# Longer allowances, an earlier division and two engines for one copy in an attention stage that a planner lays out

## The chip, the cores and the metric

The kernel runs on one core of one Trainium2 chip. The metric is the device time of one execution in microseconds (us). Of the kernel before there are three timed runs and one profiled execution. TensorE is called PE here, VectorE DVE, ScalarE ACT, GpSimd POOL and SyncE SP, as in the profile; PEld is PE's weight load and SPq is SP as it issues DMAs.

## What is computed

One token mixer over 2048 tokens of width 576: sliding-window attention with 32 heads of width 18 and a window of 256, times a gate that comes from a gMLP.

```python
def _A_ref(x, wqkv, wo):                  # H = 32, Dh = 18, W = 256
    q, k, v = ...                         # x @ wqkv, by heads
    scores = einsum("bhqd,bhkd->bhqk", q, k) * (Dh ** -0.5)
    mask = (i - j >= 0) & (i - j < W)
    p = softmax(where(mask, scores, -1e9))
    o = einsum("bhqk,bhkd->bhqd", p, v)
    return o.transpose(0, 2, 1, 3).reshape(B, S, D) @ wo

def _B_ref(x, w_in, w_sp, b_sp, w_out):
    z = gelu(x @ w_in)
    z1, z2 = z[..., :Fh], layernorm(z[..., Fh:])
    g = einsum("ts,bsf->btf", w_sp, z2) + b_sp[None, :, None]
    return (z1 * g) @ w_out

xn = layernorm(x)
return x + _A_ref(xn, ...) * silu(_B_ref(xn, ...))
```

## The kernel before

The program has five stretches: the projections to q, k, v and z2; the attention stage (about 425 to 875 us of the span); the output projection `wo`; the large product with `w_sp`; and the product with `w_out`. Products are computed with operands split into a high and a low part, three matmuls for one. The change touches the attention stage alone.

**Units.** Attention runs over 16 units (`UNITS`, numbered 0 to 15, `NU` = 16): four heads by one half of the tokens each. The q and k rows of two heads (a pair, two per unit) lie in one of six slots, the tiles `att0` to `att5`. Eight DMAs per pair bring them from `st_d` (L552, `pair_jobs`). `open_unit(u)` runs when all scores of unit u-1 have been laid out; it spaces the loads for unit u+2 by `LOAD_STEP` = 700 ns and notes in `head_ready` that a pair may be used `LOAD_NS` after its last load. Unit 0 opens three pairs (3, 4, 5) at once, with an extra delay.

**What a unit does.** `max_item` (L619, L623) computes scores of 128 queries against up to 384 keys, and VectorE takes their maxima. `max_split` and `max_turn` (L634, L643, L649) turn the unit's maxima round into the tile `mhl`, and four small DMAs put them into the slots as two more rows (L656). `scores` (L751, L755) computes the scores once more, transposed and with the maxima taken off, and ScalarE takes the exponential into `pt`. GpSimd zeroes the corners of `pt` that lie outside the window (the masks, `affine_select`, L764 and L767). `pv` (L780) multiplies by the values into the bank `ops`, which ScalarE copies to `ou` (L795). `finish` then divides by the sums of the exponentials: the sums go out as `den` (L852), VectorE inverts them (L825), they go to `r_d` (L827) and come back spread over partitions into the tile `rp` (L832; there is one `rp` buffer for units 0 to 14), GpSimd multiplies in four parts (L836), and four DMAs store the rows to `o_d` (L841). `INVERT_AT`, `FETCH_AT` and `DIVIDE_AT` say when, counted from the unit's end. The last unit but one (14) has shorter delays, and the last (15) is divided in the next stretch.

**Fill.** Between those, PE computes the product z1 of the gMLP (`z1_rows`, L696): 18 blocks of weights (`z1raw`, L666, split on ScalarE and GpSimd at L712), two halves of the array's rows that work side by side, 27 matmuls to a bank. When a bank is complete ScalarE copies it to one of three `z1o` buffers (L701), and SP stores that to `z1_d` (L590; the profile calls it `z_d`), `KEEP_NS` later in the plan.

**What sets the order.** The whole stage is laid out by a planner that runs while the program is built. It keeps a clock and, for each engine, the time until which it is busy (`use`, `busy`), at estimated costs; it gives PE the next thing whose inputs it takes to be ready, `GUARD` ns after their estimated end: a `pv` run, a turn of maxima, a score, a maximum, or else a z1 matmul. DMAs and delayed work wait in a list (`after`, `tick`). The result is one fixed order for each engine. On the chip each engine follows its order and waits for semaphores, SP too: a DMA that must wait holds all DMAs behind it. DMAs take eight semaphores in turn, so a DMA also waits until the eighth before it has landed.

Of the kernel before, what the change touches and what calls it, by code (L numbers as in the profile page):

```python
# [11 lines left out]
AF = mybir.ActivationFunctionType  # L12
# [19 lines left out]
HS = S // 2  # L32
SLOT = HS + HS + 256
UNITS = [(g, half) for half in range(2) for g in range(8)]
NU = len(UNITS)
# [4 lines left out]
RMN = 16  # L40
QR = 5
STEPS = 27
GUARD = 150
LOAD_NS = 7500
MAX_NS = 8500
KEEP_NS = 2000
LOAD_STEP = 700
INVERT_AT = 11000
FETCH_AT = 8000
# [19 lines left out]
def kernel(  # L69
# [14 lines left out]
    act, dve, pool, pe, sp = nc.scalar, nc.vector, nc.gpsimd, nc.tensor, nc.sync  # L84
# [14 lines left out]
    r_d = dram.tile([NU, 4, HS], F32, name="r_d")  # L99
# [139 lines left out]
    with ExitStack() as early:  # L239
# [282 lines left out]
        with ExitStack() as ph:  # L522
# [34 lines left out]
            clock = 0.0  # L557
            row_time = [0.0, 0.0]

            def after(ns, fn):  # L560
                waiting.append((clock + ns, fn))
# [19 lines left out]
            def use(engine, ns, drain=0):  # L581

                busy[engine] = max(busy[engine], clock + 200) + ns
                return busy[engine] + drain
# [79 lines left out]
            def load_z1(f):  # L664
                raw = zw.tile([P, 9, P], F32, name="z1raw", bufs=1)
                sp.dma_start(raw, w_z1[f])  # L666
                wh, wl = (zw.tile([P, 9, P], F32R, name=n) for n in ("z1wh", "z1wl"))

                jobs = []
                for ks in (slice(0, 3), slice(3, 6), slice(6, 9)):  # L670
                    jobs.append((partial(act.activation, wh[:, ks], raw[:, ks], AF.Copy), "act", 420))
                for ks in (slice(0, 3), slice(3, 6), slice(6, 9)):
                    jobs.append((partial(pool.tensor_tensor, wl[:, ks], raw[:, ks], f32(wh[:, ks]), ALU.subtract),
                                 "pool", 1000))
                return wh, wl, jobs

            z1w = {}
# [5 lines left out]
            def z1_rows(r):  # L683

                for f in range(FH // P):
                    z1_at[r] = f
                    if f not in z1w:
                        z1w[f] = load_z1(f)
                    wh, wl, jobs = z1w[f]
                    while jobs:  # L690
                        jobs.pop(0)[0]()
                    for b in range(2):
                        bank, ps = take()
                        bank_of[r] = bank
                        for n, (w, x_) in enumerate(moving_x(wh, wl, slice(b * 512, (b + 1) * 512), r)):
                            pe.matmul(ps, w, x_, start=n == 0, stop=n == STEPS - 1)  # L696
                            spend(r, MM + 3)
                            z1_done[r] += 1
                            if n == STEPS - 1:
                                zo = zw.tile([P, 512], F32, name="z1o", bufs=3)  # L700
                                act.activation(zo, ps, AF.Copy)  # L701
                                bank_of[r] = None
                                bank_free[bank] = use("act", 480, 120) + 100
                                after(bank_free[bank] - clock + KEEP_NS,
                                      partial(sp.dma_start, z1_tokens[f * P:(f + 1) * P, b, :, r],
                                              zo.rearrange("p (a q) -> p a q", a=2)))
                            if f + 1 < FH // P and min(z1_at) == f:
                                if b == 0 and n == 0 and f + 1 not in z1w:
                                    z1w[f + 1] = load_z1(f + 1)
                                if b == 1 and n % 4 == 2 and f + 1 in z1w and z1w[f + 1][2]:  # L710
                                    job, engine, ns = z1w[f + 1][2].pop(0)
                                    job()  # L712
                                    use(engine, ns)
                            yield
# [21 lines left out]
            def scores(u, kb, qa, qz, j):  # L736
                half = UNITS[u][1]
                lo = 8 * half
                base = 0 if half == 0 else 6
                if (u, kb) not in pts:  # L740
                    pts[u, kb] = ap_.tile([P, 4, 384], F32, name="pt", bufs=PTB)
                    left[u, kb] = 4
                pt = pts[u, kb]
                left[u, kb] -= 1
                n = qz - qa + 1
                a = qa
                if n == 1:
                    a = qa - 1 if qa > lo else qa
                m = max(n, 2)
                bank, ps = take()  # L750
                pe.matmul(ps[:, :m * P], k_of(u, j)[:, (kb - base) * P:(kb - base + 1) * P],  # L751
                          q_of(u, j)[:, (a - lo) * P:(a - lo + m) * P], start=True, stop=True)
                spend(j % 2, MM * m / 4 + 4)
                d0 = (qa - kb) * P
                act.activation(pt[:, j, d0:d0 + n * P], ps[:, (qa - a) * P:(qa - a + n) * P], AF.Exp, scale=scale)  # L755
                done_exp.append(use("act", 53 + 106 * n, 125))
                bank_free[bank] = done_exp[-1] + GUARD
                if not left[u, kb]:
                    todo.append([done_exp[-1] + 200, u, kb, qa, qz])
                    for cut in (qa == kb, qz == kb + 2):  # L760
                        busy["pool"] = max(busy["pool"], todo[-1][0]) + 600 * cut
                    todo[-1][0] = busy["pool"] + 100
                    if qa == kb:
                        pool.affine_select(out=pt[:, :, 0:P], in_=pt[:, :, 0:P], pattern=[[0, 4], [1, P]],  # L764
                                           compare_op=ALU.is_ge, fill=0.0, base=0, channel_multiplier=-1)
                    if qz == kb + 2:
                        pool.affine_select(out=pt[:, :, 256:384], in_=pt[:, :, 256:384], pattern=[[0, 4], [-1, P]],  # L767
                                           compare_op=ALU.is_gt, fill=0.0, base=0, channel_multiplier=1)
# [40 lines left out]
            def finish(u, ou):  # L809
# [6 lines left out]
                def rp():  # L816
# [4 lines left out]
                                  f32(slots[4][:, 0:HS]))  # L821
                    return at[0]

                def invert():
                    dve.reciprocal(den, den)  # L825
                    t = use("dve", 270) - clock + 300
                    after(t + (1500 if u < NU - 2 else 300), lambda: sp.dma_start(r_d[u].rearrange("h (a b) -> (h a) b", b=HS // 32), den))  # L827
                    for i in range(4):
                        after(t + (FETCH_AT if u < NU - 2 else 4500) + 400 * i, partial(sums, i))

                def sums(i):
                    sp.dma_start(rp()[32 * i:32 * i + 32, :], r_d[u][i:i + 1, :].to_broadcast([32, HS]))  # L832
# [1 line left out]
                def divide(a, n=4):  # L834
                    hs = slice(a * HS // n, (a + 1) * HS // n)
                    pool.tensor_tensor(ou[:, hs], ou[:, hs], rp()[:, hs], ALU.mult)  # L836
                    use("pool", 2900 / n)

                def store(i):
                    h = 4 * g + i  # L840
# [2 lines left out]
                if u == NU - 1:  # L843
                    def put_last():
                        dve.reciprocal(den, den)
                        sp.dma_start(r_d[u].rearrange("h (a b) -> (h a) b", b=HS // 32), den)

                    last.extend([lambda: sp.dma_start(den, ou[DH::32, :]), put_last,
                                 lambda: [sums(i) for i in range(4)], lambda: [divide(a, 2) for a in range(2)],
                                 lambda: [store(i) for i in range(4)]])  # L850
                else:
                    after(busy["act"] - clock + 1000, lambda: sp.dma_start(den, ou[DH::32, :]))  # L852
                    sooner = 10000 if u == NU - 2 else 0
                    after(4500 if sooner else INVERT_AT, invert)
                    parts[u] = [partial(divide, a) for a in range(4)] + [partial(store, i) for i in range(4)]
                    for ns in DIVIDE_AT:
                        after(ns - (14500 if sooner else 0), partial(part, u))

            def sp_combos(stack):

# [180 lines left out]
            with ExitStack() as heads:  # L1041
# [23 lines left out]
                def open_unit(u):  # L1065

                    pairs = (2 * u + 4, 2 * u + 5) if u else (3, 4, 5)
                    jobs = [(p, it) for p in pairs if p < 2 * NU for it in [pair_jobs(p)] for _ in range(8)]
                    for i, (p, it) in enumerate(jobs):
                        ns = 300 + LOAD_STEP * i + (4000 if u == 0 else 0)  # L1070
                        after(ns, partial(next, it, None))
                        head_ready[p] = clock + ns + LOAD_NS

# [680 lines left out]
```

## Time and profile before

| | |
|---|---|
| median of 3 runs | 1839.44 us (1839.17 to 1839.54) |
| profiled execution, its own time | 1837.79 us |
| its span, from first to last instruction | 1836.0 us |
| granted TensorE clock, mean | 0.994 |
| first and last z1 matmul of the attention stage (PE) | 425.4 and 872.3 us |
| POOL busy, in all | 430.5 us (23%) |

The page's first part gives each engine's busy time and share. Its second part cuts the span into 40 slices; PE is at 9 tenths in all but a few, among them those at about 440, 600 and 850 us. The windows ask for the same by chosen stretches: columns are the stretch, its length, then busy time and number of instructions of PE, PEld, DVE, ACT and POOL, then the granted PE clock, the DMA engines' share and GB/s. Matmuls overlap in PE, so a window of 10.00 busy can still hide gaps shorter than a matmul's 0.4 us. A row of the waits reads: engine, tile and line, what it waited for, us in total, times, longest. In a timeline the last bracket gives the idle time before an instruction and what ended it.

### The profile page before, as it was taken

To read this page: it belongs to the slowest core of one execution; us is meant where nothing else is said; L and a number is where in the kernel's file an instruction comes from. 1 tells how busy PE (TensorE), PEld (TensorE's weight loads), DVE (VectorE), ACT (ScalarE), POOL (GpSimd) and SP (SyncE) were. 2 spreads that over 40 slices of the span, in tenths; PEclk is the share of its full clock that TensorE was granted. 3 is DMA by queue.
4 is the path that set the end of the run, shared out by engine and by line. 5 is a ranking of instruction groups with operands and counts; after the bars stand their busy time and mean duration, and the time that the engine had idled before them with its cause. 6 is when DMAs were issued, how large, how long until landed. Compare 5 with 4: busy or idle time off the path is not lost.

```text
span 1836.0 us, 37716 instructions
## 1 busy us (share of the span) xinstructions
PE 1806.0 (98%) x14373; PEld 1591.3 (87%) x14373; DVE 1127.9 (61%) x2299; ACT 938.6 (51%) x1757; POOL 430.5 (23%) x507
## 2 busy tenths in 40 slices
PE   8999999999999999998999999999999999999998
PEld 8999999998778777776988888888888888899998
DVE  7321333457577666751266687667876567767876
ACT  5433322223767666775467565465454544444443
POOL 3332333343455555665000000112100000000000
PEclk9999999999999999999999999999999999999999
DMA  8785688887567777755867777699786556787554
GB/s 276 188 227 170 227 277 285 279 263 245 156 168 192 192 192 189 200 150 163 269 233 233 251 222 265 238 306 307 239 270 233 179 186 198 249 263 208 154 160 136
DMA packets 266917, 405.73 MB, mean 221 GB/s; under 512 B 52336, under 2 KB 180592, under 8 KB 266608
## 3 DMA queue, kind: packets, MB, share of 16 engines
q1 hardware_dynamic: 266736, 403.32, 71.7%
q8 instruction: 113, 1.85, 0.4%
q14 instruction: 68, 0.56, 0.1%
HBM read 285.35 MB, written 117.09 MB: 219 GB/s over the span
## 4 chain that ended last, share of the span: by engine, by line
PE 83%; DMA 6%; DVE 5%; SPq 2%; ACT 2%; issue 1%; POOL 1%; DVEq 0%; ACTq 0%; POOLq 0%
PE acc L1493 34%; PE mb L209 11%; PE c L1585 8%; PE ma L209 5%; PE ops L780 4%; PE s L696 3%; PE wops L1212 3%; PE t L696 3%; PE mb L696 2%; PE ma L696 2%; SPq L366 1%; PE s L619 1%; DMA att<-st_d 1%; DMA st_d<-qkhl 1%; DMA wraw<-in_w_qk_dram 1%
## 5 line engine op out<-in xcount | busy, mean ns | idle before, releaser
L1493 PE MATMUL acc<-spl,zh 128*128 128x512 f32 x1008 | 392.6, 390 | 0.9 <-DVE spl L119 0.5
L1493 PE MATMUL acc<-sph,zl 128*128 128x512 f32 x1008 | 392.2, 389 | 0.0
L1493 PE MATMUL acc<-sph,zh 128*128 128x512 f32 x1008 | 392.1, 389 | 0.0
L119 DVE TENSOR_TENSOR spl<-spr,sph 128x1024 fp32r<-128x1024 f32 x168 | 210.2, 1251 | 39.4 <-ACT sph L118 37.7
L1493 PEld LDWEIGHTS acc<-spl,zh 128*128 128x128 f32 x1008 | 189.2, 188 | 41.7 <-DVE spl L119 2.6
L1493 PEld LDWEIGHTS acc<-sph,zh 128*128 128x128 f32 x1008 | 189.2, 188 | 39.6
L1493 PEld LDWEIGHTS acc<-sph,zl 128*128 128x128 f32 x1008 | 189.2, 188 | 38.9
L118 ACT ACTIVATE zh<-b 128x384 fp32r<-128x384 f32 x168 | 87.4, 520 | 209.9 <-PE acc L1493 209.8
L118 ACT ACTIVATE sph<-spr 128x1024 fp32r<-128x1024 f32 x168 | 176.0, 1048 | 13.0 <-DMA spr<-in_w_sp_dram 5.3
L119 DVE TENSOR_TENSOR zl<-b,zh 128x384 fp32r<-128x384 f32 x168 | 99.6, 593 | 124.5 <-ACT zh L118 124.5
L623 DVE CUSTOM_DVE_ANT_0 s<-s,band 128x384 f32<-128x384 f32 (+2 forms) x256 | 136.6, 560 | 47.8 <-PE s L619 31.8
L696 PE MATMUL s<-b,z1wh 64*128 64x512 f32 x504 | 148.6, 397 | 0.2 <-ACT z1wh L712 0.2
L1585 PE MATMUL c<-b,o 128*128 128x288 f32 x1056 | 144.6, 296 | 1.7 <-DVE o L119 0.9
L1585 PEld LDWEIGHTS c<-b,o 128*128 128x128 f32 x1056 | 141.8, 189 | 2.2 <-DVE o L119 1.1
L987 DVE BATCH_NORM_STATS2 st<-zt 128x6 f32<-128x384 f32 x96 | 49.3, 548 | 131.5 <-ACT zt L986 131.1
L755 ACT ACTIVATE pt<-s 128x384 f32<-128x384 f32 (+2 forms) x252 | 108.4, 462 | 37.8 <-PE s L751 25.3
L696 PE MATMUL t<-b,z1wh 64*128 64x512 f32 x378 | 124.3, 403 | 0.0
L209 PE MATMUL ma<-z2w,b 64*128 64x384 f32 x648 | 116.1, 333 | 0.0
L209 PE MATMUL mb<-z2w,b 64*128 64x384 f32 x648 | 116.0, 333 | 0.0
L209 PE MATMUL mb<-att,b 64*128 64x384 f32 x648 | 112.8, 331 | 0.0
L209 PE MATMUL ma<-att,b 64*128 64x384 f32 x648 | 112.8, 331 | 0.0
L209 PEld LDWEIGHTS mb<-z2w,b 64*128 64x128 f32 x648 | 112.4, 184 | 0.0
(260 smaller groups left out, 4797.8 us busy)
## 6 DMA issues: line engine op xcount, KB each, us to landing
spr<-sc_d SPq DMA_DIRECT2D x96, 512.0 KB
spr<-in_w_sp_dram SPq DMA_DIRECT2D x72, 512.0 KB
zr<-z_d SPq DMA_DIRECT2D x144, 192.0 KB
z_d<-zt SPq DMA_DIRECT2D x48, 384.0 KB
z_d<-z1o SPq DMA_DIRECT2D x72, 256.0 KB
z1t<-z_d SPq DMA_DIRECT2D x72, 256.0 KB
y_d<-z1t SPq DMA_DIRECT2D x72, 256.0 KB
a<-in_w_sp_dram SPq DMA_DIRECT2D x64, 256.0 KB
```

Of the source, the lines that this page charges most:

```text
L118: act.activation(hi, src, AF.Copy)
L119: dve.tensor_tensor(lo, src, f32(hi), ALU.subtract)
L209: pe.matmul(banks[h][:, :n], *both[h][i], start=i == 0, stop=i == STEPS - 1)
L366: sp.dma_start(rows[c].rearrange("i h a p -> (i h) a p"), f32(hl[64 * n:64 * n + 64, c]).rearrange("q (a p) -> q a p", a=2))
L623: dve.tensor_tensor_reduce(out=ps[:, :w], in0=ps[:, :w], in1=band[:, m0:384], scale=1.0, scalar=-3.0e38, op0=ALU.add, op1=ALU.max, accum_o ...
L696: pe.matmul(ps, w, x_, start=n == 0, stop=n == STEPS - 1)
L755: act.activation(pt[:, j, d0:d0 + n * P], ps[:, (qa - a) * P:(qa - a + n) * P], AF.Exp, scale=scale)
L780: pe.matmul(o_ps[c][32 * j:32 * j + 32, (qa - 4 * c) * P:(hi - 4 * c + 1) * P], vgs[u][:, kb - k0, j * VW:j * VW + 32], pt[:, j, (qa - kb) ...
L987: dve.bn_stats(st2[:, s, pc, :], zv)
L1212: pe.matmul(po[:, i, :288], lt[:, cs], r[:, i * 288:(i + 1) * 288], start=n == 0, stop=n == len(pl) - 1)
L1493: pe.matmul(acc[j], z[:, ps], w[:, cs], start=s == i == 0 and n in OPENS, stop=s == 7 and i == 2, skip_group_check=True)
L1585: pe.matmul(banks[key][:, :288], y, w, start=begin and k == n == 0, stop=close and k == 8 and n == 2, skip_group_check=True)
```

## The change

It changes estimates and delays of the planner, lets a z1 copy go to either of two engines, and gives unit 13 (the third last) delays of its own:

- `GUARD` 150 to 200 ns, `LOAD_NS` 7500 to 9500 ns, and the extra delay of unit 0's loads 4000 to 7000 ns.
- Estimated costs on GpSimd: a mask 600 to 640 ns, a quarter of a weight split 1000 to 1020, a unit's division 2900 to 2960.
- A finished z1 bank is copied by VectorE when the planner expects that to end sooner (its cost taken as 620, ScalarE's as 480).
- `early` is 0 for units 0 to 12 and 15, 1 for unit 13, 2 for unit 14. Unit 14 keeps its delays. Unit 13 is inverted 7000 ns after its end instead of 11000, its inverted sums are fetched 6000 ns after that instead of 8000, and its divisions and stores come 8000 ns sooner.

```diff
-GUARD = 150
-LOAD_NS = 7500
+GUARD = 200
+LOAD_NS = 9500
...
-                                act.activation(zo, ps, AF.Copy)
                                 bank_of[r] = None
-                                bank_free[bank] = use("act", 480, 120) + 100
+                                if max(busy["dve"], clock + 200) + 620 < max(busy["act"], clock + 200) + 480:
+                                    dve.tensor_copy(zo, ps)
+                                    bank_free[bank] = use("dve", 600, 140) + 100
+                                else:
+                                    act.activation(zo, ps, AF.Copy)
+                                    bank_free[bank] = use("act", 480, 120) + 100
...
-                        busy["pool"] = max(busy["pool"], todo[-1][0]) + 600 * cut
+                        busy["pool"] = max(busy["pool"], todo[-1][0]) + 640 * cut
...
+                early = max(u - NU + 4, 0) if u < NU - 1 else 0
+
                 def invert():
                     dve.reciprocal(den, den)
                     t = use("dve", 270) - clock + 300
-                    after(t + (1500 if u < NU - 2 else 300), lambda: sp.dma_start(r_d[u]...
+                    after(t + (1500, 600, 300)[early], lambda: sp.dma_start(r_d[u]...
                     for i in range(4):
-                        after(t + (FETCH_AT if u < NU - 2 else 4500) + 400 * i, partial(sums, i))
+                        after(t + (FETCH_AT, 6000, 4500)[early] + 400 * i, partial(sums, i))
...
-                    use("pool", 2900 / n)
+                    use("pool", 2960 / n)
...
-                    sooner = 10000 if u == NU - 2 else 0
-                    after(4500 if sooner else INVERT_AT, invert)
+                    after((INVERT_AT, 7000, 4500)[early], invert)
...
-                        after(ns - (14500 if sooner else 0), partial(part, u))
+                        after(ns - (0, 8000, 14500)[early], partial(part, u))
...
-                        ns = 300 + LOAD_STEP * i + (4000 if u == 0 else 0)
+                        ns = 300 + LOAD_STEP * i + (7000 if u == 0 else 0)
```

Since the planner decides everything by its clock, the order of all engines differs from the opening of the stage to its end. The instructions are the same, but for 15 of the 72 z1 copies, which are now on VectorE. Three places follow, in the words of the built program (line, operation, output and inputs, shape; the line numbers of the changed kernel are up to five higher).

SP at the opening of the stage, right after the values of unit 0 (`vg`); `att_6802` is the slot of pair 3, `mhl` holds unit 0's maxima, `z1o` a finished z1 bank. Before:

```order
L666 DMA z1raw<-in_w_z_dram 128x1152
L552 DMA att_6802<-st_d 36x1024
L552 DMA att_6802<-st_d 18x1024 x2
L552 DMA att_6802<-st_d 36x1024
L656 DMA att_2212<-mhl 2x8x128 x2
L656 DMA att_2213<-mhl 2x8x128 x2
L552 DMA att_6802<-st_d 36x1024
L552 DMA att_6802<-st_d 18x1024 x2
L590 DMA z_d<-z1o 128x2x256
```

Now:

```order
L666 DMA z1raw<-in_w_z_dram 128x1152
L656 DMA att_2212<-mhl 2x8x128 x2
L656 DMA att_2213<-mhl 2x8x128 x2
L552 DMA att_6802<-st_d 36x1024
L552 DMA att_6802<-st_d 18x1024 x2
L590 DMA z_d<-z1o 128x2x256 x2
L552 DMA att_6802<-st_d 36x1024 x2
```

The maxima stand ahead of pair 3's eight loads, and the first two z1 stores after three of these instead of seven and eight.

POOL at the end of the stage, with buffer numbers; `ou_13389` is unit 13's result before and `ou_13822` unit 14's, now `ou_13519` and `ou_13925`. Before:

```order
L836 TENSOR_TENSOR ou_13389<-ou_13389,rp_13996 128x256 x4
L764 AFFINE_SELECT pt_14054<-pt_14054 128x4x128
L767 AFFINE_SELECT pt_14054<-pt_14054 128x4x128
L836 TENSOR_TENSOR ou_13822<-ou_13822,rp_14081 128x256
L764 AFFINE_SELECT pt_14098<-pt_14098 128x4x128
L767 AFFINE_SELECT pt_14098<-pt_14098 128x4x128
L836 TENSOR_TENSOR ou_13822<-ou_13822,rp_14081 128x256
L764 AFFINE_SELECT pt_14137<-pt_14137 128x4x128
L836 TENSOR_TENSOR ou_13822<-ou_13822,rp_14081 128x256 x2
L764 AFFINE_SELECT pt_14168<-pt_14168 128x4x128
```

Now, two pieces of the same queue:

```order
L842 TENSOR_TENSOR ou_13519<-ou_13519,rp_13831 128x256 x2
L771 AFFINE_SELECT pt_13959<-pt_13959 128x4x128
L842 TENSOR_TENSOR ou_13519<-ou_13519,rp_13831 128x256
L768 AFFINE_SELECT pt_13980<-pt_13980 128x4x128
L771 AFFINE_SELECT pt_13980<-pt_13980 128x4x128
L842 TENSOR_TENSOR ou_13519<-ou_13519,rp_13831 128x256
```

```order
L771 AFFINE_SELECT pt_14141<-pt_14141 128x4x128
L768 AFFINE_SELECT pt_14179<-pt_14179 128x4x128
L768 AFFINE_SELECT pt_14214<-pt_14214 128x4x128
L842 TENSOR_TENSOR ou_13925<-ou_13925,rp_14221 128x256 x4
L842 TENSOR_TENSOR att5_13914<-att5_13914,att4_6804 128x512 x2
```

Unit 13's divisions have moved ahead of the last unit's masks, and unit 14's behind all of them. The last row is unit 15, divided in the next stretch.

PE at the end of the z1 matmuls; each bank belongs to one half of the array's rows. Before, the last matmuls of bank `s0` with the last one of `ma` ahead of them:

```order
L696 MATMUL ma_14252<-b2_93,z1wl_13746 128x512
L696 MATMUL s0_14263<-b2_93,z1wl_13746 128x512
L696 MATMUL s0_14263<-b2_93,z1wh_13745 128x512
L696 MATMUL s0_14263<-b5_96,z1wh_13745 128x512
L696 MATMUL s0_14263<-b2_93,z1wl_13746 128x512
```

Now the last matmul of `ma` and the first of those of `t1` behind it:

```order
L696 MATMUL ma_14105<-b2_93,z1wl_13618 128x512
L696 MATMUL t1_14272<-b1_92,z1wl_13618 128x512
L696 MATMUL t1_14272<-b1_92,z1wh_13617 128x512
L696 MATMUL t1_14272<-b4_95,z1wh_13617 128x512
L696 MATMUL t1_14272<-b1_92,z1wl_13618 128x512
```

After the first matmul of the remaining half, which runs beside the last one of `ma`, three stood alone before; now there are fifteen.

More of the change, by code (lines that the diff above doesn't have):

```diff
@@ L673, in load_z1 @@
                     jobs.append((partial(pool.tensor_tensor, wl[:, ks], raw[:, ks], f32(wh[:, ks]), ALU.subtract),
-                                 "pool", 1000))
+                                 "pool", 1020))
                 return wh, wl, jobs
@@ L826, in invert @@
                     t = use("dve", 270) - clock + 300
-                    after(t + (1500 if u < NU - 2 else 300), lambda: sp.dma_start(r_d[u].rearrange("h (a b) -> (h a) b", b=HS // 32), den))
+                    after(t + (1500, 600, 300)[early], lambda: sp.dma_start(r_d[u].rearrange("h (a b) -> (h a) b", b=HS // 32), den))
                     for i in range(4):
-                        after(t + (FETCH_AT if u < NU - 2 else 4500) + 400 * i, partial(sums, i))
+                        after(t + (FETCH_AT, 6000, 4500)[early] + 400 * i, partial(sums, i))
                 def sums(i):
```

## The prediction

> **What bounds the kernel now.** I read the page first, then the windows of 10 us over the attention stage, then the waits, the chain and single engines' timelines.
>
> ```profile
> PE 1806.0 (98%) x14373; PEld 1591.3 (87%) x14373; DVE 1127.9 (61%) x2299; ACT 938.6 (51%) x1757; POOL 430.5 (23%) x507
> PE 83%; DMA 6%; DVE 5%; SPq 2%; ACT 2%; issue 1%; POOL 1%; DVEq 0%; ACTq 0%; POOLq 0%
> ```
>
> TensorE (PE) is the bound: busy 98% of the span, 83% of the chain. The change removes no matmul, so it can only win PE's idle time and time at a low clock, and only in the attention stage (about 425 to 875 us), since the rest of the program stands as before. In the windows the second column is PE's busy time, the first of the last three is the granted clock.
>
> ```profile
> 430.00:440.00 10.00, 9.53 (x84) 8.61 (x80) 7.33 (x26) 2.73 (x7) 2.89 (x3) 1.00 0.82 215
> 440.00:450.00 10.00, 7.21 (x51) 6.51 (x53) 5.34 (x22) 0.88 (x2) 2.01 (x3) 0.83 0.78 222
> 450.00:460.00 10.00, 9.64 (x90) 8.83 (x88) 9.44 (x41) 4.87 (x11) 3.80 (x5) 1.00 0.71 224
> ...
> 540.00:550.00 10.00, 9.59 (x116) 6.36 (x109) 4.87 (x21) 3.89 (x12) 4.88 (x8) 1.00 0.82 230
> ...
> 600.00:610.00 10.00, 7.80 (x78) 6.36 (x76) 3.21 (x14) 8.53 (x21) 8.26 (x13) 1.00 0.71 184
> ...
> 640.00:650.00 10.00, 8.99 (x92) 6.62 (x92) 6.58 (x26) 4.34 (x15) 5.72 (x9) 1.00 0.88 225
> ...
> 850.00:860.00 10.00, 5.80 (x68) 3.20 (x69) 1.22 (x1) 3.27 (x12) 6.85 (x10) 0.88 0.48 144
> 860.00:870.00 10.00, 10.00 (x80) 6.05 (x74) 0.00 (x0) 1.79 (x3) 2.82 (x5) 0.78 0.55 169
> 870.00:880.00 10.00, 8.11 (x48) 6.97 (x45) 3.50 (x5) 3.51 (x4) 0.00 (x0) 0.83 0.87 270
> ```
>
> Four places stand out: the opening (440 to 450), 600 to 610, the stage's end (850 to 870), and the step into the output projection (870 to 880). What PE waited for there:
>
> ```profile
> PE ops L780 <- POOL pt L767: 4.9, 2, 4.2
> PE mb L619 <- ACT z1o L701: 2.7, 1, 2.7
> PE s L619 <- DMA att<-st_d: 2.2, 1, 2.2
> PE wops L1212 <- ACT ohl L1198: 1.9, 1, 1.9
> ```
>
> **The change part by part.** The opening: PE waits for a bank that ScalarE is to empty into z1o. ScalarE waits for its z1o buffer (there are three), so for an earlier store of z1o.
>
> ```profile
> 439.38 1.82 SPq L552 DMA_DIRECT2D att<-st_d  x3
> 441.34 0.39 SPq L590 DMA_DIRECT2D z_d<-z1o  x1
> ```
> ```profile
> 444.22 0.60 ACT L701 ACTIVATE z1o<-mb 128x512 f32<-128x512 f32 x1 [3.94 <-DMA z_d<-z1o]
> ```
> ```profile
> 433.07 8.20 DMA att<-st_d
> ```
>
> The chain's row shows a head's transfer of 8.20 us, released at 441.3, and only then does SP issue the z1o store, behind seven heads' transfers and four of maxima. With unit 0's heads begun 3 us later (4000 to 7000 ns) the order puts the maxima first and three heads' transfers before the two stores. Idle of 10.00 - 7.21 = 2.79 us goes, and the low clock after it, 10 x (1 - 0.83) = 1.7 us, of which I count 1.5 since it began in the idle time. The 0.47 and 0.36 us beside it I leave as they are. **Gain 4.3 us**, bounds 0 (the three buffers run dry again) and 0.47 + 2.79 + 0.36 + 1.7 = 5.3.
>
> At 600 to 610 the first maxima of unit 8 wait for their heads:
>
> ```profile
> 602.50 6.11 DMA att<-st_d
> ```
>
> Such a transfer takes 6.11 us. The longer allowance (7500 to 9500 ns) moves a pair's first maximum back by 2.0 us. In the order, 112 matmuls stand between unit 5's last score, which frees the slot, and unit 8's first maximum; now 137, 18 of the added ones being z1 matmuls. The wait was 2.2 us: **gain 2.0 us**, bounds 0 and 2.2. No unit has less distance than before, so I see no new wait of this kind.
>
> The end: two masks of the last unit stand on GpSimd behind divisions.
>
> ```profile
> 850.03 3.34 POOL L836 TENSOR_TENSOR ou<-ou,rp 128x256 f32<-128x256 f32 x4 [1.32 <-issue]
> ...
> 853.90 0.65 POOL L767 TENSOR_SCALAR_AFFINE_SELECT pt<-pt 128x512 f32<-128x512 f32 x1
> 857.67 0.73 POOL L836 TENSOR_TENSOR ou<-ou,rp 128x256 f32<-128x256 f32 x1 [3.12 <-DMA rp<-r_d]
> 858.35 0.64 POOL L764 TENSOR_SCALAR_AFFINE_SELECT pt<-pt 128x512 f32<-128x512 f32 x1
> 858.93 0.64 POOL L767 TENSOR_SCALAR_AFFINE_SELECT pt<-pt 128x512 f32<-128x512 f32 x1
> ```
> ```profile
> 846.40 8.70 SPq L832 DMA_DIRECT2D rp<-r_d  x5
> ```
> ```profile
> 859.63 2.37 PE ops L780 x16
> ```
>
> Unit 13's four divisions end at 853.4; only then may unit 14's sums be loaded into rp (one buffer, so SP's issues stretch over 8.70 us), and unit 14's first division waits 3.12 us for them with two masks behind it. In the changed order the first of unit 13's divisions has fifteen masks behind it, the last twelve, and all four of unit 14 come after the last mask. The idle 10.00 - 5.80 = 4.20 us goes, and the low clock that followed: PE began again at 859.63, so nearly all of it counts from 860 on, 10 x (1 - 0.78) = 2.2, and 0.2 before. **Gain 6.6 us**, bounds 0 and 4.20 + 1.2 + 2.2 = 7.6.
>
> What that costs: unit 13's sums now have 5.0 us between the planned last load and the first division, instead of 7.0 (worked out from the delays in the code: 20.0 - 7.0 - 0.8 - 6.0 - 1.2, and 28.0 - 11.0 - 0.8 - 8.0 - 1.2). Divisions elsewhere already wait for such loads, with masks behind them:
>
> ```profile
> L836 POOL TENSOR_TENSOR ou<-ou,rp 128x256 f32<-128x256 f32 x60 | 43.6, 746 | 30.6 <-DMA rp<-r_d 18.6 <-DMA att<-mhl 5.9 <-DMA z_d<-z1o 4.8
> L764 POOL TENSOR_SCALAR_AFFINE_SELECT pt<-pt 128x512 f32<-128x512 f32 x128 | 81.9, 642 | 105.8 <-ACT pt L755 101.7 <-issue 3.9
> L712 POOL TENSOR_TENSOR z1wl<-z1raw,z1wh 128x384 fp32r<-128x384 f32 x51 | 51.3, 1026 | 20.0 <-PE t L619 12.9 <-ACT z1wh L712 7.1
> ```
>
> PE lost 0.41 us at 540 to 550 and 1.01 at 640 to 650 where that happened, so I charge one more such place: **loss 0.7 us**, bounds 0 and 4.2, the last unit's price. The same rows show that the planner's new costs (640, 2960/4 = 740, 1020) are what the chip takes (642, 746, 1026); 20 to 40 ns an instruction only moves work by a place, so nothing, bounds 1.4 us either way, the two windows just named.
>
> At the very end the two row halves finish less evenly: the last 15 z1 matmuls stand alone in one half, before it was three.
>
> ```profile
> 431.76 0.40 PE L696 MATMUL mb<-b,z1wh 64*128 64x512 f32 x1
> 431.93 0.40 PE L696 MATMUL t<-b,z1wh 64*128 64x512 f32 x1
> 431.99 0.39 PE L696 MATMUL mb<-b,z1wh 64*128 64x512 f32 x1
> ```
>
> One half starts a matmul every 0.23 us with the other half's between, so 12 more alone cost 12 x 0.115 = **1.4 us**, bounds 0 (the other half did its share earlier) and 1.4. The projection's first matmul still waits for ScalarE's last z1o copy and then ohl: its 1.89 us stay.
>
> GUARD (150 to 200 ns) and 15 of the 72 z1 copies going to VectorE I cost at nothing: other z1 matmuls cover a bank that comes 50 ns later, and VectorE is busy 61%. A VectorE copy of 128x512 is not in this stage's trace; it lies between
>
> ```profile
> L649 DVE COPY mhl<-s x14: 206/217/218, 433.1 to 820.4; 64x64 f32<-64x64 f32 x14
> L1442 DVE TENSOR_TENSOR cb<-acc,t x36: 679/692/692, 1097.0 to 1629.0; 128x512 f32<-128x512 f32 x36
> ```
>
> 0.217 and 0.692 us, nearer the second. Without cover each copy holds the maxima behind it by that: 15 x 0.692 = 10.4 us; and at best PE keeps the 2.7 us of the waits for z1o, counted already.
>
> **Sum:** 4.3 + 2.0 + 6.6 - 0.7 - 1.4 = 10.8 us off the profiled execution of 1837.79 (span 1836.0), so 1827.0. The median, 1839.44, stands 1.65 above that execution, so I forecast 1828.6.
>
> The clock after a wait decides 1.5 + 2.4 = 3.9 us of this. The windows show it at 0.83 round an idle time of 2.79 us and of 1.89, but at 1.00 round 2.20: length alone doesn't decide. The Trainium skill, "TensorE: Matmul & The Clock Gate", Part 1, says that the clock is halved after an idle window of about 3.4 us, and that the windows run free. By a whole idle window the opening would keep full clock and the sum would lose its 1.5 us (an estimate, 1830.1); the 0.83 measured there speaks against reading it so strictly, and the free phase agrees with the 2.20 us that went unpunished.
>
> **The rivals.** *Half is given back* (0.22): at the opening the z1 stores still queue behind 24 heads' transfers, so the 4.3 stay lost: 1828.6 + 4.3 = 1832.9. For it: three buffers only; against: the stores move ahead in SP's order. *The waits move on* (0.08): with PE's idle time spread anew over other units, the sum comes to nothing: 1839. For it: every engine's order from the opening on is new; against: the heads' distance grows in all units. *VectorE's queue* (0.14), the slower side: VectorE takes its work in order, and a z1 copy there waits for its last matmul while maxima stand behind, on which PE's banks hang. If each of the 15 holds VectorE for two maxima of 0.591 us beyond cover, that is 17.7 us, less 10.8: 1846. It decides from 10.8 / 15 = 0.72 us a copy. The longest-standing case of such a wait on ScalarE:
>
> ```profile
> ACT z1o L701 <- PE s L696: 7.4, 3, 7.0
> L623 DVE CUSTOM_DVE_ANT_0 s<-s,band 128x384 f32<-128x384 f32 x195 | 110.8, 591 | 40.6 <-PE s L619 25.4 <-PE t L619 9.1 <-PE ma L619 5.0
> ```
>
> Against it: only three such waits in that row, and the planner gives VectorE a copy only when it expects it free sooner. That the copies don't reach VectorE at all is excluded by the order.
>
> **How the numbers follow.** Forecast 0.56, with a range of its own from 1824 to 1832. Within 0.2% (3.7 us, about what a measurement of this kernel tells from no change) lie "the waits move on" and little else. Faster: 0.56 + 0.22 less a little for overlap = 0.76; same 0.10; slower 0.14. The low end is the forecast with all upper bounds (5.3 + 2.2 + 7.6 + 1.4 + no losses = 16.5, so 1823), a little below for the wait of ScalarE's banks: 1822. The high end takes in half given back and no change: 1840; beyond it is the VectorE case.
>
> **What would show it.** Right: the opening's window without a wait of z1o for its store and clock 1.00; no wait of L619 for att<-st_d over 0.5 us; no division between the last unit's masks, and 850 to 870 at clock 1.00; a wait of 1.9 us for ohl as before. Wrong: PE waiting for VectorE's maxima or copies in the waits, a GpSimd division of unit 13 waiting over 4 us for rp, or a new window with under 9 us of PE work between 460 and 840.

## The result, and the profile after

| | before | after |
|---|---|---|
| median, same chip | 1839.32 us (4 runs, 1839.17 to 1839.54) | 1828.39 us (4 runs, 1826.50 to 1831.16) |
| profiled execution, its own time | 1837.79 us | 1826.50 us |
| its span | 1836.0 us | 1824.4 us |
| first and last z1 matmul of the stage | 425.4 and 872.3 us | 423.9 and 860.4 us |

The ratio is 0.9942, with a 95% interval from 0.9924 to 0.9959: 10.9 us off, 10.8 forecast. Two of the four executions after took 1826.5 us and two 1830.3 and 1831.2, so the median lies where none of them does. Of the span's 11.6 us, 10.4 lie between the first and the last z1 matmul (446.9 and 436.5 us) and 1.5 came before the stage, where nothing was changed; 0.3 were lost behind it. So the total came out as predicted; its parts did not.

The page after, engines and chain:

```profile
PE 1798.9 (99%) x14373; PEld 1589.3 (87%) x14373; DVE 1129.3 (62%) x2314; ACT 931.9 (51%) x1742; POOL 427.7 (23%) x507
PE 83%; DMA 7%; DVE 5%; ACT 2%; SPq 2%; issue 1%; POOL 0%; ACTq 0%; DVEq 0%; POOLq 0%
```

PE's count is the same. The windows that stood out before, and two new ones (columns as before: PE's busy time second, its granted clock first of the last three):

```profile
430.00:440.00 10.00, 9.58 (x87) 8.97 (x84) 8.08 (x34) 2.64 (x6) 3.42 (x4) 1.00 0.77 217
440.00:450.00 10.00, 8.39 (x72) 7.79 (x72) 2.27 (x9) 1.86 (x4) 0.06 (x1) 1.00 0.83 215
450.00:460.00 10.00, 7.79 (x62) 6.58 (x64) 8.48 (x36) 5.05 (x12) 4.21 (x6) 1.00 0.79 232
560.00:570.00 10.00, 8.10 (x88) 5.67 (x84) 4.46 (x20) 4.81 (x15) 5.96 (x10) 1.00 0.88 225
570.00:580.00 10.00, 10.00 (x102) 7.36 (x104) 5.92 (x26) 6.35 (x16) 3.36 (x5) 0.83 0.69 206
600.00:610.00 10.00, 10.00 (x96) 9.85 (x96) 8.46 (x31) 8.84 (x21) 7.29 (x11) 1.00 0.77 240
850.00:860.00 10.00, 10.00 (x110) 6.89 (x100) 0.00 (x0) 3.03 (x9) 4.36 (x7) 1.00 0.40 124
860.00:870.00 10.00, 7.70 (x42) 6.98 (x41) 3.50 (x5) 4.10 (x5) 0.00 (x0) 0.83 0.83 255
```

The end is full at 850 to 860 and 600 to 610 is full. The opening has not been mended: from 430 to 460 PE idles 0.42 + 1.61 + 2.21 = 4.24 us, before it was 0.47 + 2.79 + 0.36 = 3.62; only the low clock is gone. And at 560 to 570 there is a new gap. PE's waits in the stage name the two:

```profile
PE s L619 <- DVE z1o L703: 2.9, 1, 2.9
PE t L755 <- DMA att<-mhl: 1.9, 1, 1.9
PE wops L1217 <- ACT ohl L1203: 1.8, 1, 1.8
PE mb L619 <- ACT z1o L706: 1.4, 1, 1.4
```

At the opening the engine has changed, the cause has not: VectorE's copy waits for a z1o buffer, so for a store that SP issued between heads' transfers, and the maxima wait behind it. VectorE's timeline, then SP's:

```profile
451.45 0.69 DVE L703 COPY z1o<-s 128x512 f32<-128x512 f32 x1 [7.81 <-DMA z_d<-z1o]
452.06 0.29 DVE L623 CUSTOM_DVE_ANT_0 s<-s,band 128x128 f32<-128x128 f32 x1
```
```profile
444.43 1.04 SPq L590 DMA_DIRECT2D z_d<-z1o  x2
445.52 7.72 SPq L552 DMA_DIRECT2D att<-st_d  x10
453.98 1.12 SPq L590 DMA_DIRECT2D z_d<-z1o  x2
```

The new gap, from the chain inside 560 to 575 (start, us, what) with the SP timeline behind it:

```profile
558.72 4.04 DMA att<-st_d
...
563.52 5.56 DMA att<-mhl
...
569.22 0.41 PE t L755
```
```profile
562.82 3.57 SPq L656 DMA_DIRECT2D att<-mhl  x4
```

In the view of the tile `mhl` its last copy by VectorE starts at 557.1:

```profile
L649 DVE COPY mhl<-mb x1: 205/205/205, 557.1 to 557.1; 64x64 f32<-64x64 f32 x1
```

So `mhl` was complete 5.5 us before its four transfers were issued, from 562.8 on; they stood behind heads' transfers on SP and landed at 569.1; PE idled 1.9 us for them and then ran at 0.83 of the clock for a window.

### The profile page after: what moved, and what is told of

The parts are those of the page before. It is cut to its first block, busy times and chain, and to the rows that moved or that the text cites. A ratio compares the mean times of both kernels' runs of the same rounds, so it can differ in the third digit from the quotient of the medians.

```text
span 1824.4 us, 37719 instructions
## 1 busy us (share of the span) xinstructions
PE 1798.9 (99%) x14373; PEld 1589.3 (87%) x14373; DVE 1129.3 (62%) x2314; ACT 931.9 (51%) x1742; POOL 427.7 (23%) x507
## 4 chain that ended last, share of the span: by engine, by line
PE 83%; DMA 7%; DVE 5%; ACT 2%; SPq 2%; issue 1%; POOL 0%; ACTq 0%; DVEq 0%; POOLq 0%
PE acc L1498 35%; PE mb L209 11%; PE c L1590 8%; PE ma L209 5%; PE s L696 5%; PE ops L784 4%; PE t L696 3%; PE wops L1217 3%; PE ma L696 2%; PE mb L696 1%; SPq L366 1%; PE s L619 1%; DMA wraw<-in_w_qk_dram 1%; PE s L755 1%; DMA st_d<-qkhl 1%
## 5 line engine op out<-in xcount | busy, mean ns | idle before, releaser
L119 DVE TENSOR_TENSOR spl<-spr,sph 128x1024 fp32r<-128x1024 f32 x168 | 210.3, 1252 | 39.5 <-ACT sph L118 37.9
L119 DVE TENSOR_TENSOR zl<-b,zh 128x384 fp32r<-128x384 f32 x168 | 98.8, 588 | 123.3 <-ACT zh L118 123.2
L623 DVE CUSTOM_DVE_ANT_0 s<-s,band 128x384 f32<-128x384 f32 (+2 forms) x244 | 130.6, 559 | 46.7 <-PE s L619 24.2
L696 PE MATMUL s<-b,z1wh 64*128 64x512 f32 x522 | 155.1, 396 | 0.0
```

What stands on the lines that cost most here:

```text
L119: dve.tensor_tensor(lo, src, f32(hi), ALU.subtract)
L623: dve.tensor_tensor_reduce(out=ps[:, :w], in0=ps[:, :w], in1=band[:, m0:384], scale=1.0, scalar=-3.0e38, op0=ALU.add, op1=ALU.max, accum_o ...
```

## The experiments

Twelve kernels ran on three further chips, four on each; the kernel before ran beside them and gave medians of 1836.80, 1836.45 and 1835.96 us. Behind each time stands its ratio to that kernel with the 95% interval; differences in us are taken from the ratios, so those between kernels of different chips rest on the kernel before as their ruler. I sought the cause of the end's gain first, since the prediction tied it to one order of divisions, and the price of the edits I had costed at nothing.

**e1: GUARD undone.**

```diff
-GUARD = 200
+GUARD = 150
```

> The changed kernel with GUARD back at 150 ns. Theory G: the 50 ns are what shortened PE's small waits for banks all through the stage (weight loads waiting for ScalarE's exponentials: 9.0 us over 26 waits before, 2.8 us over 10 now, in the middle of the stage). Then the time goes up by 3 to 6 us, to 1831.5 to 1834.5, and those waits are back near 8 us. Rival R: the small waits fell because the z1 copies that VectorE took relieve ScalarE, or because any new order falls out differently; then the time stays within 1.5 us of 1828.4, or moves without those waits rising.

Measured: 1832.64 us, 0.9973 [0.9960, 0.9986], against 0.9942 [0.9924, 0.9959] for the whole change: 5.7 us of the gain gone, or 3.7 against the changed kernel's second measurement (e5, 0.9953 [0.9935, 0.9971]), whose interval overlaps this one. That agrees with G in size, but not in its sign: between 470 and 830 us weight loads waited 4.5 us for ScalarE's exponentials, not near 8. Its divisions stand behind the last masks and its end has no such wait, so this loss is not the end's.

**e2: GUARD alone.** The kernel before with:

```diff
-GUARD = 150
+GUARD = 200
```

> The kernel before with GUARD at 200 ns and nothing else. Theory G: 3 to 6 us off, 1833.5 to 1836.5, with the weight loads' waits for exponentials near 3 us in the middle of the stage. Rival R: 1838 to 1841 and those waits still near 9 us.

Measured: 1832.11 us, 0.9970 [0.9957, 0.9983], 5.5 us faster. In its order unit 14's four divisions have moved behind the last mask, without any edit to unit 13 or 14, and the 4.2 us wait for a mask is gone from 850 to 860. PE has a new wait of 2.0 us near 840, for ScalarE's `ou`, and at the opening it still waits for z1o 2.7 us as before. Theory G's sign is missing here too: weight loads waited 5.3 us for exponentials between 470 and 830, where 3 was expected.

**e3: the changed kernel with unit 13's old delays.**

```diff
-                early = max(u - NU + 4, 0) if u < NU - 1 else 0
+                early = 2 if u == NU - 2 else 0
```

> The changed kernel with unit 13's own delays taken out (unit 14 keeps its own). The plan is the same up to unit 13's end. Theory E: the end's wait of two masks for unit 14's sums is back, with the low clock behind it, and costs 4 to 7 us: 1832.5 to 1835.5, all of it after 830 us of the span. Rival: the longer allowances had already pulled the end apart, so it costs under 1.5 us.

Measured: 1829.16 us, 0.9954 [0.9938, 0.9970]. The wait at the end did not come back. A miss for the theory that unit 13's earlier division had removed it: in this plan too unit 14's divisions stand behind all masks. The time is the rival's: beside e5 (0.9953) nothing was lost.

**e4: the kernel before with unit 13's new delays alone.**

```diff
-                    after(4500 if sooner else INVERT_AT, invert)
+                    after((INVERT_AT, 7000, 4500)[early], invert)
...
-                        after(ns - (14500 if sooner else 0), partial(part, u))
+                        after(ns - (0, 8000, 14500)[early], partial(part, u))
```

> The kernel before with unit 13's delays and nothing else. Everything up to about 800 us as before. Theory E: 4 to 7 us off, 1832.5 to 1835.5, PE busy in the windows from 840 to 870 with clock 1.00. Rival: unit 13's earlier division waits for its own sums with masks behind it, and gives back 3 us or more: over 1836.

Measured: 1834.38 us, 0.9985 [0.9970, 0.9999], 2.8 us off (0.2 to 5.5), less than theory E's 4 to 7, though the interval reaches into it. GpSimd's timeline and PE's wait at the end:

```profile
853.53 0.72 POOL L838 TENSOR_TENSOR ou<-ou,rp 128x256 f32<-128x256 f32 x1 [3.26 <-DMA rp<-r_d]
854.21 0.64 POOL L764 TENSOR_SCALAR_AFFINE_SELECT pt<-pt 128x512 f32<-128x512 f32 x1
```
```profile
PE ops L780 <- POOL pt L767: 3.1, 1, 3.1
```

Unit 13 is divided sooner, and still unit 14's first division waits 3.26 us for rp (3.12 before) with masks behind it. So the early division does not bring the sums in time; what matters is whether masks stand behind the division that waits. e8 tests that place by itself.

**e5: the changed kernel again**, unaltered, as the ruler of its chip.

> The changed kernel once more, unaltered, on the chip of the next three, as their ruler. Every theory: 0.992 to 0.997 of the kernel before. Its profile tells which waits of the first one belong to the plan and come again (two waits of 1.5 to 3.3 us for copies into z1o between 430 and 460, one of about 2 for mhl's transfer round 570, one of about 2 for ohl at 862) and which were a transfer's luck.

Measured: 1828.10 us, 0.9953 [0.9935, 0.9971], so 8.6 us off on this chip. PE's waits:

```profile
PE t L756 <- DMA att<-mhl: 3.0, 1, 3.0
PE mb L620 <- ACT z1o L707: 2.3, 1, 2.3
PE wops L1218 <- ACT ohl L1204: 1.8, 1, 1.8
PE s L620 <- DVE z1o L704: 1.1, 1, 1.1
```

(Its lines are one higher.) The same four waits as above: they belong to the plan, though their lengths change.

**e6: all copies on ScalarE.**

```diff
-                                if max(busy["dve"], clock + 200) + 620 < max(busy["act"], clock + 200) + 480:
+                                if False:
```

> The changed kernel with all 72 z1 copies on ScalarE. Theory F (the prediction's: the copies of VectorE are worth nothing): within 1.5 us of the changed kernel. Theory S (ScalarE's queue is relieved by them, and exponentials come sooner): 2 to 5 us slower, and between 470 and 830 the weight loads' wait for ScalarE's pt grows from 2.4 to 4 or more. Theory H (a copy on VectorE that waits for its buffer holds up the maxima behind it at the opening): the 1.6 us wait for VectorE's z1o near 452 is gone and nothing of its size stands in its place, 1 to 3 us faster.

Measured: 1831.37 us, 0.9976 [0.9962, 0.9990], 4.2 us slower than e5 by the ratios (3.3 by the medians), but the intervals overlap. Theory S's sign was not there (weight loads' waits for ScalarE's pt stayed at 2.2 us), nor H's: ScalarE's own copy now holds 2.5 us at the opening. Inconclusive.

**e7: the opening's transfers spread.**

```diff
-                        ns = 300 + LOAD_STEP * i + (7000 if u == 0 else 0)
+                        ns = 300 + (1300 * i + 4000 if u == 0 else LOAD_STEP * i)
```

> The changed kernel with the opening's transfers of heads 1.3 us apart from 4.3 us on in place of 0.7 apart from 7.3 us on. Theory Q (z1's stores wait behind these transfers and hold the copies' buffers): the waits of 1.6 and 2.2 us for z1o between 430 and 460 shrink to under 1.5 together, 2.5 to 4.5 us of that window. Theory L (a store lands 7 us after its issue whatever stands round it, three buffers are too few): over 2.5 us of idle stay there. At the end one division of the last unit but one now stands before the last mask, which costs 0 to 3 us there by the theory of e8; so the window decides, the total only from 3 us on.

Measured: 1829.22 us, 0.9959 [0.9945, 0.9974]. Windows of e7, opening and end:

```profile
430.00:440.00 10.00, 8.95 (x78) 7.73 (x77) 6.14 (x25) 2.32 (x6) 2.63 (x3) 1.00 0.76 209
440.00:450.00 10.00, 9.73 (x88) 9.11 (x86) 4.00 (x16) 2.56 (x5) 1.73 (x3) 1.00 0.83 222
450.00:460.00 10.00, 10.00 (x95) 9.08 (x92) 8.11 (x35) 8.02 (x20) 5.57 (x9) 1.00 0.95 276
...
850.00:860.00 10.00, 8.98 (x85) 6.52 (x74) 0.00 (x0) 1.80 (x3) 3.40 (x5) 1.00 0.44 126
860.00:870.00 10.00, 8.16 (x33) 6.76 (x33) 3.50 (x5) 2.92 (x3) 0.00 (x0) 0.72 0.87 268
```

Theory Q holds for the window: idle falls from 4.24 us (3.44 in e5) to 1.32 with the same three buffers, and of that only 0.3 us is a wait for z1o, where it was 2.9 + 1.4 (2.3 + 1.1 in e5). The total did not follow. One division stands before the last mask here and GpSimd waits 1.9 us for its rp, which shows at 850 to 860.

**e8: the place alone.** The kernel before with unit 14's divisions 4 us later; nothing ahead of 820 us moves.

```diff
-                        after(ns - (14500 if sooner else 0), partial(part, u))
+                        after(ns - (10500 if sooner else 0), partial(part, u))
```

> The kernel before with unit 14's four divisions asked for 4 us later, so that they stand behind all masks of the last unit on GpSimd; nothing ahead of 820 us moves. Theory P (place: the end's wait is there because divisions that wait for rp stand ahead of the last masks): the 4.2 us wait for POOL's mask near 855 and the low clock behind it go, 3.5 to 6.6 us faster. Rival O (what is divided later is stored and projected later): the wait for ohl behind 870 grows from 1.9 by as much as the mask's shrinks, within 1 us of before.

Measured: 1831.66 us, 0.9974 [0.9964, 0.9984]: 4.8 us (2.9 to 6.6) by one number. GpSimd's end, and the windows:

```profile
854.72 1.23 POOL L764 TENSOR_SCALAR_AFFINE_SELECT pt<-pt 128x512 f32<-128x512 f32 x2
856.62 2.83 POOL L836 TENSOR_TENSOR ou<-ou,rp 128x256 f32<-128x256 f32 x4 [0.67 <-DMA rp<-r_d]
```
```profile
850.00:860.00 10.00, 9.44 (x111) 5.63 (x110) 0.00 (x0) 3.91 (x12) 8.79 (x14) 1.00 0.56 171
860.00:870.00 10.00, 7.65 (x58) 6.03 (x55) 1.65 (x2) 2.47 (x4) 0.00 (x0) 1.00 0.79 235
```

The sums land no sooner than before, but no mask waits behind them. Theory P holds. Rival O does not hold at the first wait for ohl, which is 1.9 us as it was, but a little of it comes later. PE stops twice for the last unit's ohl, where the kernel before ran the whole projection without a stop:

```profile
898.77 0.80 PE L1212 MATMUL wops<-att,ohl 128*128 128x288 f32 x4 [0.73 <-ACT ohl L1198]
900.03 12.18 PE L1212 MATMUL wops<-att,ohl 128*128 128x288 f32 x90 [0.46 <-DVE ohl L1199]
```

The sums of the last unit (`den`) were sent out 1.5 us after the projection's first matmul (868.87 and 867.38), in the kernel before 0.8 us ahead of it (873.78 and 874.54).

**e9: e8 with the longer allowance.**

```diff
-LOAD_NS = 7500
+LOAD_NS = 9500
```

> The kernel before with unit 14's divisions behind the last masks (as in e8) and the allowance for heads' transfers of the change, 9.5 us for 7.5. Theory T (the prediction's second step): no wait for a head near 600 to 610, 1 to 3 us faster than e8's 0.9974, so 0.9958 to 0.9969. Rival J (that wait comes and goes with the transfers, and a longer allowance only lays the rest out otherwise): within 0.0007 of e8.

Measured: 1834.65 us, 0.9989 [0.9978, 1.0000]. Neither by the medians: about 2.8 us slower than e8, but the intervals overlap, so rival J is not excluded. PE's waits:

```profile
PE mb L619 <- ACT z1o L701: 2.6, 1, 2.6
PE t L619 <- ACT z1o L701: 2.0, 1, 2.0
PE t L619 <- DMA att<-st_d: 1.7, 1, 1.7
```

No wait near 600, as step two had it; but with unit 0's loads where they were, the opening gets a second wait for z1o, and a maximum of another unit (at 658 us) waits 1.7 us for its head. From 430 to 460 PE idles 5.7 us, in e8 3.4, and a second window there runs at 0.83; what the allowance did for the middle of the stage is taken up below.

**e10: e8 with the copies on either engine** (the `if` of the change, 11 of 72 on VectorE).

> The kernel before with unit 14's divisions behind the last masks and z1 copies by whichever of the two engines is free (11 of 72 on VectorE). Theory F: within 0.0007 of e8's 0.9974. Theory S: 2 to 5 us faster than e8, 0.9947 to 0.9963, and weight loads wait less for ScalarE's pt between 470 and 830 than e8's 9.8 us. Rival of the prediction (VectorE's queue): slower than e8 by 2 or more, with waits for VectorE's maxima.

Measured: 1836.97 us, 1.0006 [0.9997, 1.0016]; the interval is clear of e8's, 5.9 us slower. PE's waits, then VectorE's timeline:

```profile
PE t L696 <- ACT z1o L706: 2.8, 1, 2.8
PE s L755 <- DVE z1o L703: 2.8, 2, 2.0
PE mb L619 <- ACT z1o L706: 2.5, 1, 2.5
```
```profile
844.21 0.76 DVE L119 TENSOR_TENSOR att<-ou,att 128x576 fp32r<-128x576 f32 x1 [1.57 <-ACT att L118]
845.91 0.98 DVE L119 TENSOR_TENSOR att<-vg,att 128x576 fp32r<-128x576 f32 x1 [0.95 <-ACT att L118]
846.82 0.68 DVE L703 COPY z1o<-s 128x512 f32<-128x512 f32 x1
```

Here is the rival about VectorE's queue, in the opposite direction: a finished bank waits on VectorE behind splits (L119) that wait for ScalarE's halves, and PE waits 2.0 us for the bank. Theory S's sign was there without its gain: weight loads waited 4.8 us for ScalarE's pt between 470 and 830, in e8 9.8. The profile is of the slowest of the twelve executions (1842.89 us), so its waits explain the median only in part.

**e11: the changed kernel with the old allowance.** Its plan puts two of unit 14's divisions ahead of the last mask again.

```diff
-LOAD_NS = 9500
+LOAD_NS = 7500
```

> The changed kernel with the old allowance of 7.5 us. Its plan puts two of unit 14's divisions ahead of the last mask again, though unit 13 keeps its earlier delays. Theory P: a wait of 2.5 to 4.5 us for that mask comes back near 850, and the whole is 3 to 6 us slower than the changed kernel's 0.9953, so 0.9969 to 0.9986. Rival U (unit 13's delays removed that wait): no wait over 1.5 us there, and a total within 2 us of the changed kernel but for what the allowance is worth.

Measured: 1833.72 us, 0.9983 [0.9974, 0.9993], 5.5 us slower than e5, intervals apart. GpSimd's end and PE's wait:

```profile
856.89 1.40 POOL L842 TENSOR_TENSOR ou<-ou,rp 128x256 f32<-128x256 f32 x2 [4.10 <-DMA rp<-r_d]
858.25 0.64 POOL L768 TENSOR_SCALAR_AFFINE_SELECT pt<-pt 128x512 f32<-128x512 f32 x1
```
```profile
PE ops L784 <- POOL pt L768: 4.3, 1, 4.3
```

The wait is back, at its old length, in a kernel that has unit 13's earlier division. With e3, e4 and e8 that settles it: the place of unit 14's divisions makes the wait, not unit 13's delays. The 5.5 us are not that wait's price alone, since the shorter allowance lays the whole stage out anew; no run moves only these divisions forward in the changed kernel.

**e12: opening spread and unit 14 later.** e7 with:

```diff
-                        after(ns - (0, 8000, 14500)[early], partial(part, u))
+                        after(ns - (0, 8000, 13500)[early], partial(part, u))
```

> The changed kernel with the opening's transfers spread (e7) and unit 14's divisions asked for 1 us later, so that all four stand behind the last masks. Theory P: the waits of 1.4 us at 850 and the low clock of 0.72 behind 863 in e7 go but for ohl's 1.8, and it is 1 to 3 us faster than e7's 0.9959, so 0.9943 to 0.9954, at or below the changed kernel. Rival C (what a plan removes in one place another stall takes): within 0.0006 of e7.

Measured: 1827.12 us (1822.67 to 1829.01), 0.9946 [0.9933, 0.9959], within theory P's range; but the interval overlaps e7's, so rival C is not excluded. Its largest waits in the stage:

```profile
PE wops L1217 <- ACT ohl L1203: 1.8, 1, 1.8
PE s L755 <- ACT pt L759: 1.8, 2, 1.6
```

Nothing over 1.8 us is left there. It has the lowest median of all the kernels run, but by its ratio it is not below the changed kernel (0.9942 on the first chip, 0.9953 [0.9935, 0.9971] in e5).

## Why the prediction was right in sum and wrong in parts

- **Bound.** PE's idle time and clock in the attention stage alone: right. 10.4 of 11.6 us came from there, and the rest of the span went unchanged but for 1.5 us won ahead of the stage and 0.3 lost behind it.
- **Opening, gain 4.3: failed.** The failing step is "the order puts the maxima first and three heads' transfers before the two stores": true, but it was taken to free the buffers for good. The next stores were issued at 444.4 and 454.0 behind further heads' transfers, and PE idled 4.24 us for 3.62. Only the 1.7 us of low clock stayed away, in both profiles of the changed kernel. So about 1 us came of the 4.3. This is the mechanism of the rival "half is given back", which had a chance of 0.22; its time, 1832.9, did not come. e7 shows that the prediction had the cause right: spread the transfers, and the idle time falls to 1.32 us.
- **600 to 610, gain 2.0: right in effect, not in full as a cause.** The wait is gone in the changed kernel both times. It was also gone in e4, whose plan there is that of before, so a transfer's time alone can remove it; and e9, with the longer allowance, has a wait of 1.7 us for a head elsewhere and lost more at the opening than it won here.
- **End, gain 6.6: right in mechanism, and nearly in size.** Divisions that wait for rp ahead of the last masks: e8 gives 4.8 us (2.9 to 6.6) for removing that, and e11, where it is back, stands 5.5 behind e5. In e8's profile the way from a mask that both traces share (835.82 us, in e8 834.65) to the projection's first matmul (874.54 and 867.38) is 6.0 us shorter. Of that 0.8 is given back by the projection's last matmul (935.5 and 929.1), with the stops for ohl. In the changed kernel 850 to 860 is full at full clock; the 0.83 at 860 to 870 belongs to the step into the projection, which had 0.83 before too (870 to 880). What I held to be the edit behind it (the third last unit divided sooner) is not: e3 without it kept the gain, e4 with it alone kept the wait. Every edit that shifts the plan decides anew where these divisions fall.
- **Unit 13's sums, loss 0.7.** In the changed kernel they start (at 833.7) without a wait for rp; e3 without and e5 with the new delays gave 0.9954 and 0.9953, so they cost and bring nothing that these runs can tell.
- **Lone z1 matmuls, loss 1.4: right by the trace.** From 857.16 to 860.43 us fifteen matmuls of `t` stand alone, one every 0.23 us; before that the two halves start one each in such a time.
- **Pool costs, nothing.** Not measured apart.
- **GUARD and copies, nothing: failed as a claim.** Undoing GUARD alone leaves 0.9973 (e1), 3.7 to 5.7 us short of the whole change and no more gain than the divisions' place gives by itself (e8, 0.9974). GUARD alone gains 5.5 (e2), but with the divisions moved as in e8, which has 4.8 without it. The copies cost 5.9 us when added to e8 (e10), and taking them out of the whole brought no gain either (e6). In these runs no edit shows a price of its own: each lays the whole stage out anew. A sign of the rival "VectorE's queue" did appear: the maxima waited 2.9 us behind VectorE's copy (1.1 in e5). But that copy waited for its z1o buffer, not for its bank, and the whole did not turn slower.
- **Unforeseen:** the wait for `mhl`, 1.9 us (3.0 in e5) and a window or two of low clock. The text's condition "a new window with under 9 us of PE work between 460 and 840" named its sign, but no term did.
- **The clock.** After 1.8 to 1.9 us of waiting for ohl it was low in the changed kernel (0.83 at 860 to 870) and full in e8. By the Trainium skill, "TensorE: Matmul & The Clock Gate", Part 1, only a whole idle window of about 3.4 us should halve it. In these runs 1.8 us of waiting was enough. That the windows run free, as the same part of the Trainium skill says, agrees with the chance.

That the sum came right is luck: some 3 of the opening's 4.3 us were not gained and 3.6 were lost at `mhl` (1.9 and 1.7 of clock), and gains that no term had counted made up for them. Between 470 and 830 us PE ran 38 matmuls more than before (windows of before and after):

```profile
470.00:830.00 360.00, 354.88 (x3731) 1.00 0.68 182
```
```profile
470.00:830.00 360.00, 357.14 (x3769) 1.00 0.69 182
```

These are 65 more of z1 (1566 for 1501), 31 fewer of `pv` (1229 for 1260) and 4 others. A z1 matmul takes PE 0.117 us (each half starts one every 0.23), one of `pv` about 0.06 (24 took 1.50), one of the others about 0.09 (three quarters of z1's width), so this is some 6 us, an estimate, net of the wait for `mhl` and its clock. It is spread over short waits (weight loads waited 2.4 us for ScalarE's pt there, 7.6 before; 2.8 for GpSimd's, 5.7 before). e5 ran 46 more of z1 and 44 fewer of `pv`: 2.5 us by the same prices, with 3.0 us of waiting and 3.4 of clock lost at `mhl`. Without `mhl` both come to about 9 us, of which the prediction had counted 2.0. Single profiles differ here by some 2 us: e4, whose plan is that of before, ran 6 more of z1 and 20 of `pv`.

So of the gain, 4.8 us are shown to be the divisions' place; which edits share the other 4 to 6 stays open. None alone, on top of that place, brought it: e2 with GUARD (0.9970) was level with e8, e9 and e10 came out slower. The longer allowance is a candidate, not more: e9 ran 25 more of z1, 12 of `pv` and 9 others than e8 between 470 and 830, some 4.4 us, and lost about as much at the opening, where it lacks the change's later start of unit 0's loads.

## What to carry to other kernels

When a planner fixes the order, price the places, not the constants: look up which instruction waits, what stands behind it on its engine, and move that one thing, as e8 did for 4.8 us with one number. A constant that shifts the whole plan draws every such place anew: the allowance and the copies, parts of a change that wins 9 to 11 us, came out about 3 us (within the noise) and 6 us slower when each was added alone to e8. Before counting a stall as gone, follow the queue past the first two instructions that moved: here the third store was issued at 444.4 us, 6.4 us after its copy had ended.

## What was unexpected of the hardware

Three chips scattered the unchanged kernel from 1832.3 to 1842.3 us, where the first gave 1839.17 to 1839.54; two readings of one plan differ there by more than most edits are worth. And the same 1.8 to 1.9 us wait for ohl was followed by full clock in e8, by one window at 0.83 in the changed kernel and by 0.72 in e7, so what such a wait costs can't be told from its length: a stretch at 0.83 adds 1.7 us to it, as much again. Nor does a longer one decide it: the changed kernel's 2.9 us at the opening left the clock at 1.00.
